# Row maxima that start with the first 512 keys, later zeros, and value products handed out one and a half batches per turn

## The chip, the core and the metric

The kernel runs on one core of a Trainium2 chip. The core has a matrix engine (PE; its weight loads are listed apart as PEld), a vector engine (DVE), a scalar engine (ACT), a general engine (POOL) and a queue engine (SP) that issues transfers. Transfers (DMA) can also be issued from ACT and POOL. The measure is the device time of one launch in microseconds (us); lower is better.

## The reference

For 2048 tokens `x` of width 448 the kernel computes a gated mix of an attention block and an MLP block:

```python
g = sigmoid((x * gate_w).sum(-1, keepdims=True))
q, k, v = split_heads(x @ wqkv)                 # 16 heads of 28
scores = einsum("bhqd,bhkd->bhqk", q, k) * 28 ** -0.5
a = merge_heads(softmax(scores) @ v) @ wo
y = layernorm(x)
b = gelu(y @ w1 + b1) @ w2 + b2                 # 448 -> 1792 -> 448
return g * a + (1 - g) * b
```

All data are float32. The softmax subtracts the maximum of each row of scores, so the maximum over all 2048 keys must be known before a row's exponentials are taken.

## The kernel before, in words

**Stages.** The program has three stretches. A short head loads the first inputs. The *strips* stretch computes the queries and keys (pieces `QK`), the values (`Val`) and the MLP (`Up`, then `Down`, for each of four chunks of 512 tokens). The *attention* stretch computes scores, exponentials and the products with the values, and ends with the output projection.

**Strips.** In the strips stretch PE is used as four strips of 32 rows. Four small products, one in each strip, run beside one another; a full product of 128 rows is cut into four pieces that visit the four strips. Class `Strips` is a planner that runs while the program is built: it keeps a modelled time for each strip (`t`), for DVE, ACT and POOL, and for the transfers (`get`: data at 230 GB/s, then 2.2 us), and writes the instructions in the order in which they come due. Everything that is to be done at a modelled time is put on a list with `at`. The engines then run this order at their own pace: each engine works its instructions strictly in order, and waits where an input is not there.

**Row maxima.** To have the maxima early, the scores are computed twice. The first time (`RowMax`) each of 1024 *searches* (`one`) multiplies 128 queries with 512 keys of one head in one strip (line L199), and a DVE reduction (L201) takes the maximum of each row. A search needs the keys of its head in `kd` and the queries in `qd`, both read back from DRAM, where the `QK` pieces wrote them (`qk<-qo`, issued by ACT). There are 16 rounds of 64 searches, one for each group of four heads and chunk of 512 queries. In the strips stretch searches go into strips wherever the planner finds one of the two score banks 6 and 7 free; what is left is done in the attention stretch. `hot[j]` is the modelled time from which strip j may search; `ready(j)` tells whether its keys are loaded.

Before the change, all four heads' whole keys (224 KB each) and queries (56 KB each) were loaded by POOL after the last key piece of all four chunks was done. For later groups the planner allowed the strip again 8.0 us after its last search with the old keys.

**Attention.** The 1024 units (128 keys by 512 queries of one head) are done in *turns* of 5 or 6 units. A turn writes, on PE: the scores of half a (three units, banks 0 to 2), those of half b (two or three units, banks 3 to 5), three products for each unit (L1121), with searches between them; then *batches* of value products (L1133), each of four units, into bank 7; then, late in the program, a piece of the output projection (L970 to L972, 12 products). ACT takes the exponentials of each half with one instruction (L1125) into a tile `p`; only then can the next turn's scores use the banks. A turn has 5 units with three searches while searches are owed, and 6 units with at most two after that: `turn_of` decides by what is left. Value batches are written as soon as the units of earlier turns make up four, so turns of six have one and two batches in turn.

**The end of the strips.** `early` prepares the attention while the last chunk of the MLP is still running: POOL zeroes `la`, fetches keys and queries and splits them into high and low parts.

## Time and profile before

| | us |
|---|---|
| median of 3 runs | 1094.24 (1091.7 to 1096.02) |
| the profiled execution, its own time | 1093.73 |
| its span | 1091.6 |
| first strip matmul / end of the strips / first exponential | 16.05 / 446.6 / 449.44 |
| searches before 449.44 us / after | 529 / 495 |

The span is what the trace covers. A *group* row gives the busy time and the mean duration of all instructions of one line; the *chain* is the path of work that ended last, followed back from the end; a row of *windows* gives, for a stretch of time, each engine's busy time and number of instructions; the *timeline* gives instructions in order of time, and in brackets the idle time ahead of one and what ended it. Several PE instructions in different strips or columns run beside one another, so PE is shown busy wherever at least one runs, and its share does not tell how many strips are filled. In the trace a float32 value product shows as two matmul instructions: a batch of four products is 8 of them.

### The profile page before, as it was taken

The page shows a single profiled execution, that of the slowest core. Times are in us where ns is not written, and L with a number is a line of the kernel's source. Part 1 is how long each engine was busy: PE and PEld are TensorE (multiplying, and loading weights), DVE is VectorE, ACT ScalarE, POOL GpSimd, SP SyncE. Part 2 cuts the span into 40 slices and gives each one's busy share as a digit, 9 for nine tenths or more (in the row PEclk, how much of TensorE's full clock was granted, in tenths as well). Part 3 has the DMA queues.
Part 4 walks back from the last instruction along what each step waited for, and adds up shares of the span by engine and source line. Part 5 has one row for each costly group of instructions (what it writes and reads, how often), then busy time and mean ns, then how long its engine had stood idle before and what let it go on. Part 6 is the DMA issues. An engine that isn't in the chain of part 4 may idle for free.

```text
span 1091.6 us, 30496 instructions
## 1 busy us (share of the span) xinstructions
PE 1074.6 (98%) x13170; PEld 724.8 (66%) x13170; DVE 739.2 (68%) x1186; ACT 634.8 (58%) x668; POOL 364.1 (33%) x372
## 2 busy tenths in 40 slices
PE   9999999999999999999999999999999999999998
PEld 7989999999999999644444444444444444354555
DVE  4289989998999998667666766566767666321102
ACT  5324472141151150588878878878878878858562
POOL 3546687345242057321100110310012215345441
PEclk9999999999999999999999999999999999999999
DMA  6795433104100105410000000400002101011111
GB/s 231 225 293 190 167 120 109 43 5 103 38 9 11 38 9 127 119 40 27 18 14 19 22 23 25 117 17 16 19 18 73 38 16 54 25 52 38 61 52 59
DMA packets 47462, 73.15 MB, mean 67 GB/s; under 512 B 13632, under 2 KB 28608, under 8 KB 46416
## 3 DMA queue, kind: packets, MB, share of 16 engines
q1 hardware_dynamic: 33888, 39.11, 12.4%
q0 software_dynamic: 4800, 16.89, 5.4%
q10 hardware_dynamic: 8640, 15.21, 3.9%
q8 instruction: 103, 1.69, 0.6%
q14 instruction: 31, 0.25, 0.1%
HBM read 51.75 MB, written 19.31 MB: 65 GB/s over the span
## 4 chain that ended last, share of the span: by engine, by line
PE 93%; ACT 2%; DVE 2%; issue 1%; DMA 1%; POOL 0%; DVEq 0%; ACTq 0%
PE bk L475 33%; PE bk L1133 22%; PE bk L1121 18%; PE bk L199 15%; ACT p L1125 2%; PE bk L970 1%; DVE mx L201 1%; PE bk L971 1%; PE bk L972 1%; PE bk L886 1%; DMA qk<-qo 1%; PE bk L871 0%; DVE ob L992 0%; POOL hl L350 0%; DVE acc L977 0%
## 5 line engine op out<-in xcount | busy, mean ns | idle before, releaser
L201 DVE TENSOR_REDUCE mx<-bk 128x1 f32<-128x512 f32 x1024 | 672.4, 689 | 202.8 <-PE bk L199 157.0
L1125 ACT ACTIVATE p<-bk 128x1536 f32<-128x1536 f32 (+1 forms) x395 | 482.1, 1276 | 142.2 <-PE bk L1121 142.2
L199 PE MATMUL bk<-kd,qd 28*128 28x512 f32 x1024 | 446.7, 437 | 3.7 <-issue 1.4
L199 PEld LDWEIGHTS bk<-kd,qd 28*128 28x128 f32 x1024 | 186.1, 182 | 196.9 <-DVE mx L201 131.8
L475 PE MATMUL bk<-yh,w1f 32*128 32x512 f32 x1568 | 183.0, 391 | 0.4 <-ACT gb L385 0.4
L475 PE MATMUL bk<-yl,w1f 32*128 32x512 f32 x784 | 161.0, 391 | 0.0
L475 PEld LDWEIGHTS bk<-yh,w1f 32*128 32x128 f32 x1568 | 151.8, 183 | 2.2 <-ACT gb L385 1.7
L475 PE MATMUL bk<-w2h,hh 32*128 32x448 f32 x896 | 133.2, 366 | 1.3 <-ACT hh L343 1.3
L475 PE MATMUL bk<-w2l,hh 32*128 32x448 f32 x896 | 132.5, 363 | 0.0
L1133 PE MATMUL bk<-p,va 128*32 128x512 f32 x1024 | 131.2, 602 | 0.0
L1133 PE MATMUL bk<-p,vb 128*32 128x512 f32 x1024 | 129.5, 601 | 0.0
L350 POOL TENSOR_TENSOR hl<-h,hh 128x512 fp32r<-128x512 f32 x56 | 73.7, 1325 | 132.2 <-ACT hh L343 71.2
L806 POOL CAST yh<-yl 128x512 fp32r<-128x512 f32 x16 | 9.8, 614 | 293.6 <-PE bk L1133 118.4
L1121 PE MATMUL bk<-yh,ka 29*128 29x512 f32 x512 | 107.0, 482 | 0.3 <-ACT h L385 0.3
L475 PEld LDWEIGHTS bk<-yl,w1f 32*128 32x128 f32 x784 | 103.6, 183 | 0.2
L1121 PE MATMUL bk<-yh,kb 29*128 29x512 f32 x512 | 98.1, 477 | 3.8 <-ACT p L1125 3.5
L475 PEld LDWEIGHTS bk<-w2h,hh 32*128 32x128 f32 x896 | 99.5, 183 | 1.9 <-ACT hh L343 1.7
L475 PEld LDWEIGHTS bk<-w2l,hh 32*128 32x128 f32 x896 | 100.4, 183 | 0.1
L1121 PE MATMUL bk<-yh,la 28*128 28x512 f32 x512 | 88.5, 393 | 0.0
L385 ACT ACTIVATE gb<-bk 128x448 f32<-128x448 f32 x14 | 7.6, 545 | 138.3 <-PE bk L475 133.3
L475 PE MATMUL bk<-w2h,hl 32*128 32x448 f32 x896 | 87.3, 362 | 0.0
L1121 PE MATMUL bk<-yl,ka 28*128 28x512 f32 x512 | 86.9, 410 | 0.0
(141 smaller groups left out, 1591.3 us busy)
## 6 DMA issues: line engine op xcount, KB each, us to landing
qk<-qo ACTq DMA_DIRECT2D x28, 256.0 KB
raw<-in_xt SPq DMA_DIRECT2D x17, 256.0 KB
vs<-vt ACTq DMA_DIRECT2D x16, 256.0 KB
rc<-rls SPq DMA_DIRECT2D x60, 64.0 KB
bxr<-in_xk POOLq DMA_DIRECT2D x8, 448.0 KB, 6.4
acc<-gbs SPq DMA_DIRECT2D x16, 224.0 KB
out_y<-acc SPq DMA_DIRECT2D x16, 224.0 KB
qd<-qk SPq DMA_DIRECT2D x60, 56.0 KB
```

Source lines behind the costliest of these rows:

```text
L199: nc.tensor.matmul(ps, self.qd[n % 2][r, i * P:(i + 1) * P], self.kd[r, k * 512:(k + 1) * 512], start=True, stop=True)
L201: nc.vector.reduce_max(self.mx[n % 2][:, j, i, k:k + 1], ps, axis=AX)
L350: nc.gpsimd.tensor_sub(hl[f], h, hh[f].bitcast(F32))
L475: mm = nc.tensor.matmul(bk[:, x.bank, :n], a, b, start=x.first, stop=(len(x.rem) == 1 and m == len(ops) - 1), skip_group_check=True)
L806: nc.gpsimd.tensor_copy(h, l.bitcast(F32))
L886: nc.tensor.matmul(bk[:, b], w, v, start=(i == 0), stop=(i == len(ops) - 1), skip_group_check=True)
L970: nc.tensor.matmul(po, h, woh[:, g], start=(g == 0), stop=False, skip_group_check=True)
L971: nc.tensor.matmul(po, h, wol[:, g], start=False, stop=False, skip_group_check=True)
L972: nc.tensor.matmul(po, l, woh[:, g], start=False, stop=(g == NG - 1), skip_group_check=True)
L1121: nc.tensor.matmul(bk[:, turn_bank(i)], w[r, ks], q[r], start=(p == 0), stop=(p == 2), skip_group_check=True)
L1125: nc.scalar.activation(t[:, :count], bk[:, b:b + count], AF.Exp, scale=SCALE)
L1133: nc.tensor.matmul(bk[32 * j:32 * j + 32, 7], vg[n // NC][:, k, 32 * j:32 * j + 32], prob.pop(4 * b + j), start=(k == 0), stop=(k == NT - ...
```

## The change

1. **Key blocks.** `load_block(c)` loads the 512 keys of chunk c for the four heads of the first group (four transfers of 28x512, 56 KB each) on POOL's queue. It is called 4.0 us (modelled) after the strips begin for chunk 0, together with the first queries, and for each later chunk 5.0 us after the two pieces that hold those keys. The first round goes through the keys outermost, so that it can begin with one block; `ready` lets it go as far as `blocks` says.
2. **Allowed from the modelled landing.** For later groups `hot[j]` is set when the keys' transfer is issued, to its modelled landing plus 1.0 us, and the transfer is entered in the planner's model of the transfers.
3. **Zeros later.** In `early`, the zeroing of `la` moves from 0.5 to 4.0 us after the last `Up` piece, the key fetches by 2.5 us and their splits by 1.5 us.
4. **Half batches.** In a turn of six, value work is limited to a quota of 3 halves (4 when more than two batches are behind). A batch may be cut into two halves of 256 columns, the second of which is written in the next turn.

```diff
         def ready(self, j):
-            n = self.cnt[j] // 16
+            n, x = divmod(self.cnt[j], 16)
+            if n == 0:
+                return x // 4 < self.blocks
...
-            i, k = divmod(x, 4)
+            i, k = divmod(x, 4) if n else divmod(x, 4)[::-1]
...
                 elif kind == "k":
-                    self.at(now + 1.5, lambda n=n, j=j: rowmax.load_k(n, j))
-                    self.hot[j] = now + 8.0
+                    def load(n=n, j=j):
+                        rowmax.load_k(n, j)
+                        self.hot[j] = self.get(self.clock + 0.6, 224) + 1.0
+
+                    self.at(now + 1.5, load)
+                    self.hot[j] = 1e9
...
+            if x.i in (3, 4) and all((x.c, m) in st.qks for m in (3, 4)):
+                keys(st, x.c, now + 5.0)
             if not st.keyed and all((c, m) in st.qks for c in range(NC) for m in (3, 4)):
                 st.keyed = True
-                def first(j):
-                    rowmax.load_k(0, j, nc.gpsimd)
-                    rowmax.load_q(0, j, nc.gpsimd)
...
+    def keys(st, c, when):
+
+        def load():
+            if c == 0:
+                for j in range(4):
+                    rowmax.load_q(0, j, nc.gpsimd)
+                    st.use("pool", st.clock, 0.55)
+                    st.get(st.pool, 56)
+            rowmax.load_block(c, nc.gpsimd)
+            st.use("pool", st.clock, 0.6)
+            st.at(st.get(st.pool, 230) + 1.0, landed)
+
+        def landed():
+            rowmax.add_block()
+            st.hot = [min(x, st.clock) for x in st.hot]
+
+        st.at(when, load)
...
+        keys(st, 0, 4.0)
...
-        st.at(now + 0.5, lambda: nc.gpsimd.memset(la.bitcast(F32), 0.0), pool=2.2)
+        st.at(now + 4.0, lambda: nc.gpsimd.memset(la.bitcast(F32), 0.0), pool=2.2)
...
-    def batch(b, turn):
+    def batch(b, turn, sl=slice(0, CH)):
...
-        before = u
+        before, quota = u, 99
         if u < UNITS:
             u += turn_of(u, turn)
+            if u - before == 6:
+                quota = 3 + (before // 4 - b > 2)
...
-        while 4 * b + 4 <= before:
-            b += 1
-            if batch(b - 1, turn):
+        while 4 * b + 4 <= before and quota:
+            if quota == 1 and not begun_half:
+                if b % NT:
+                    batch(b, turn, slice(0, CH // 2))
+                    begun_half = True
+                break
+            last = batch(b, turn, slice(CH // 2 if begun_half else 0, CH))
+            quota -= 1 if begun_half else 2
+            b, begun_half = b + 1, False
+            if last:
                 break
```

What this does to the order of the instructions is shown at three places. The first is POOL's queue early in the strips stretch: `first` and `raw` are landing buffers for inputs and weights, `bxr` those of the layer statistics, `wq` the split weights of the `QK` pieces. Before:

```order
L554 DMA first_136<-in_xt 128x512
L554 DMA first_137<-in_wqk 128x512
L554 DMA raw_130<-in_wqk 128x512
L96 TENSOR_TENSOR wq_526<-first_137,wq_526 128x384
L97 TENSOR_TENSOR wq_526<-first_137,wq_526 64x128
L96 TENSOR_TENSOR wq_549<-raw_130,wq_549 128x384
L97 TENSOR_TENSOR wq_549<-raw_130,wq_549 64x128
L554 DMA bxr_147<-in_xk 128x2x448
L554 DMA bxr_148<-in_xk 128x2x448
L554 DMA raw_131<-in_wqk 128x512
```

Now, from the same transfer on:

```order
L571 DMA first_136<-in_xt 128x512
L196 DMA qd_150<-qk 28x512 x4
L186 DMA kd<-qk 28x512 x4
L571 DMA first_137<-in_wqk 128x512
L571 DMA raw_130<-in_wqk 128x512
L96 TENSOR_TENSOR wq_536<-first_137,wq_536 128x384
L97 TENSOR_TENSOR wq_536<-first_137,wq_536 64x128
L96 TENSOR_TENSOR wq_561<-raw_130,wq_561 128x384
L97 TENSOR_TENSOR wq_561<-raw_130,wq_561 64x128
L186 DMA kd<-qk 28x512 x4
L571 DMA bxr_147<-in_xk 128x2x448
L571 DMA bxr_148<-in_xk 128x2x448
```

Twenty small loads now stand among the early transfers (a row with x4 is four of them): four of queries and four of the first key block ahead of the next weights, and a block of four ahead of the statistics' inputs, twice more further down. Before, eight loads (four of 28x2048 keys, four of 28x512 queries) stood together further down the queue, behind the loads of two later sets of `QK` weights.

The second place is PE in the attention stretch, where turns of six without searches stand. `yh`, `yl` are the split queries, `kb`, `lb` the split keys, `vb` the values, `p` the exponentials. Before, with the value batches of one turn (four products), the scores of the next, and its batches (eight products):

```order
L1133 MATMUL bk<-p_15797,vb 32x512
L1133 MATMUL bk<-p_15832,vb 32x512 x3
L1121 MATMUL bk<-yh,kb 128x512 x3
L1121 MATMUL bk<-yh,lb 128x512 x3
L1121 MATMUL bk<-yl,kb 128x512 x3
L1121 MATMUL bk<-yh,kb 128x512 x3
L1121 MATMUL bk<-yh,lb 128x512 x3
L1121 MATMUL bk<-yl,kb 128x512 x3
L1133 MATMUL bk<-p_15843,vb 32x512 x3
L1133 MATMUL bk<-p_15866,vb 32x512 x3
L1133 MATMUL bk<-p_15877,vb 32x512 x2
```

Now, from the second part of one turn's value work on (half a batch of 256 columns), the scores of the next turn, and its value work (half a batch and a whole one):

```order
L1164 MATMUL bk<-p_15987,vb 32x256
L1164 MATMUL bk<-p_15998,vb 32x256 x3
L1152 MATMUL bk<-yh,kb 128x512 x3
L1152 MATMUL bk<-yh,lb 128x512 x3
L1152 MATMUL bk<-yl,kb 128x512 x3
L1152 MATMUL bk<-yh,kb 128x512 x3
L1152 MATMUL bk<-yh,lb 128x512 x3
L1152 MATMUL bk<-yl,kb 128x512 x3
L1164 MATMUL bk<-p_15987,vb 32x256
L1164 MATMUL bk<-p_15998,vb 32x256 x3
L1164 MATMUL bk<-p_16024,vb 32x512 x3
L1164 MATMUL bk<-p_16035,vb 32x512
```

Most turns of six (49 of 57) now have one and a half batches behind their scores, where one and two took turns. Over the whole stretch the order has 161 turns of five and 36 of six before and a last one of three units, with 495 searches; now 136 of five, 57 of six and a last one of two, with 458 searches. 28 batches are cut in two. Of the 57, 28 hold two searches.

The third place is POOL at the end of the last `Up` pieces (`hl` is the low part of the MLP's hidden layer, needed by `Down`). Before:

```order
L350 TENSOR_TENSOR hl_2821<-h,hh_2807 128x512
L829 MEMSET la 128x2048
L350 TENSOR_TENSOR hl_2822<-h,hh_2808 128x512
L350 TENSOR_TENSOR hl_2823<-h,hh_2809 128x512
L350 TENSOR_TENSOR hl_2824<-h,hh_2810 128x512
L802 DMA yl<-qk 28x512
L785 DMA la<-qk 28x2048
```

Now:

```order
L363 TENSOR_TENSOR hl_2912<-h,hh_2898 128x512
L363 TENSOR_TENSOR hl_2911<-h,hh_2897 128x512
L363 TENSOR_TENSOR hl_2913<-h,hh_2899 128x512
L833 DMA yl<-qk 28x512
L860 MEMSET la 128x2048
L833 DMA yl<-qk 28x512
L816 DMA la<-qk 28x2048
```

The zeroing of `la` stood ahead of the last three low parts and now stands behind them, after the first query fetch.

More of the change, by code (lines that the diff above doesn't have):

```diff
@@ L169, in __init__ @@
             self.has = set()
+            self.blocks = 0
             self.qd = [mpool.tile([P, CH], F32R, name=f"qd{i}") for i in range(2)]
@@ L180, in load_k, with load_block, add_block @@
             self.has.add((g, j))
+        def load_block(self, c, queue):
+            cs = slice(c * CH, (c + 1) * CH)
+            for j in range(4):
+                queue.dma_start(self.kd[32 * j:32 * j + DH, cs].bitcast(F32), qk[D + j * DH:D + (j + 1) * DH, cs])
+        def add_block(self):
+            self.blocks += 1
+            if self.blocks == NC:
+                self.has.update((0, j) for j in range(4))
         def load_q(self, n, j, queue=nc.sync):
@@ L736, in done @@
                 early(st, now)
+    def keys(st, c, when):
+        def load():
+            if c == 0:
+                for j in range(4):
+                    rowmax.load_q(0, j, nc.gpsimd)
[8 more added lines that the diff above has]
+        st.at(when, load)
     def enter_mlp(st, now):
```

12 lines of the change are left out of this document (5 added, 7 removed).

## Prediction

> **What bounds the kernel.** I read the page first, then the groups, then windows and the chain for each stretch.
>
> ```profile
> span 1091.6 us, 30496 instructions
> PE 1074.6 (98%) x13170; PEld 724.8 (66%) x13170; DVE 739.2 (68%) x1186; ACT 634.8 (58%) x668; POOL 364.1 (33%) x372
> DVE  4289989998999998667666766566767666321102
> PE 93%; ACT 2%; DVE 2%; issue 1%; DMA 1%; POOL 0%; DVEq 0%; ACTq 0%
> ```
>
> PE is busy everywhere and carries 93% of the chain, at the full granted clock in the windows below. So time is gained only by PE's rows being fewer, being filled better in their four strips, or not standing still. DVE is nearly full from 57 us to the end of the strips (446 us), and has room before and behind. Where searches can be done is therefore a question of DVE's room in the strips.
>
> ```profile
> 20.00:57.00 37.00, 37.00 (x628) 36.87 (x625) 8.16 (x20) 10.23 (x19) 16.52 (x27) 1.00 0.64 195
> 57.00:446.00 389.00, 384.35 (x6623) 368.90 (x6617) 363.91 (x580) 125.68 (x223) 194.12 (x186) 1.00 0.29 89
> 449.44:920.57 471.13, 378.78 (x320) 1.00 0.13 37
> 920.57:1066.60 146.03, 99.06 (x73) 1.00 0.13 43
> 920.57:1066.60 146.03, 17.26 (x44) 8.24 (x44) 1.00 0.13 43
> ```
>
> The first two rows are windows of all engines (columns: width, then busy time and count of PE, PEld, DVE, ACT, POOL). From 20 to 57 us DVE works 8.16 of 37 us: this is the hole into which the change puts searches. The next two rows count the exponentials, two to a turn: 320 of them are 160 turns in 471.13 us, 2.945 us for a turn of five, chunk changes included. The last row counts line L970, four to a piece of the output projection: 11 pieces.
>
> **Fewer and other turns.** The order has 25 turns of five fewer (161 to 136) and 21 turns of six more (36 to 57). The fives go with 25 x 2.945 = 73.6 us; between chunk changes a turn is a little shorter, as four turns in the chain show, 638.36 - 626.68 = 11.68 or 2.92 each:
>
> ```profile
> 626.68 1.85 PE bk L1133 x16
> ...
> 638.36 1.90 PE bk L1133 x16
> ```
>
> I take 2.92: 73.0 us. What a turn of six costs depends on its value batches.
>
> ```profile
> 944.07 1.85 PE bk L1133 x16
> 945.92 0.92 PE bk L1121 x11
> ...
> 948.28 1.46 ACT p L1125
> 949.77 0.51 PE bk L1121 x3
> ...
> 950.75 1.85 PE bk L1133 x16
> ...
> 957.43 1.85 PE bk L1133 x16
> ```
>
> This is the chain through two pairs of turns of six. From one double batch (x16) to the next it is 6.68 us, and in each pair the chain leaves PE: the exponentials of half b end at 949.74, and only then PE writes the next scores of half b. The turn with one batch is too short for ACT, the turn with two leaves ACT idle. Where nothing waits, the parts are these:
>
> ```profile
> 990.32 1.85 PE bk L1133 x16
> 992.18 1.60 PE bk L1121 x16
> ...
> 1013.23 0.99 PE bk L1133 x8
> ...
> 932.50 0.42 PE bk L199
> ...
> 934.22 1.00 PE bk L1133 x8
> ```
>
> Scores of six units take 1.60 us, with two searches 934.22 - 932.50 = 1.72. One batch takes 0.99, a second behind it 0.86, so half a one 0.43. A turn with one and a half batches is then 1.60 + 0.99 + 0.43 = 3.02 us, or 3.14 with two searches. ACT needs less:
>
> ```profile
> 946.93 5.48 ACT L1125 ACTIVATE p<-bk 128x1536 f32<-128x1536 f32 x4 [1.20 <-PE bk L1121]
> ```
>
> Four exponentials back to back take 5.48, 2.74 for a turn; the 1.20 us of idleness ahead of them is what an even share takes away. The scores of that turn began at 945.92, so the exponentials start 1.01 after a turn's scores and both have ended 1.01 + 2.74 = 3.75 after them. Half b of the next turn is due 3.02 + 0.92 = 3.94 after them. The banks are free 0.2 us early: little, and the reason for the second rival.
>
> Now the sum for the sixes. The window of 146.03 us holds 35 of the 36 sixes, one five and 11 projection pieces. A piece is the gap between a batch and the next scores:
>
> ```profile
> 1014.22 0.40 PE bk L970
> ...
> 1016.85 1.59 PE bk L1121 x16
> ```
>
> 2.63 us. So a six costs (146.03 - 2.92 - 11 x 2.63) / 35 = 3.26 us on the mean, 36 of them 117.4. After it 28 with two searches make 87.9 and 29 others 87.6, together 175.5. The 28 cut batches issue twice as many products; between nothing (the second half starts behind other products) and 0.13 each (what a batch that comes first pays over one that follows) that is 0 to 3.6, and I take 1.0, since a half mostly follows a whole batch. In "TensorE: Matmul & The Clock Gate", section Back-to-back issue gap, the Trainium skill gives 518 cycles for 512 columns and 262 for 256, so that cutting would cost 6 cycles a product; by that this term would be about 0.1 and the time 0.9 lower. No run here shows a product of 256 columns. Attention: 175.5 + 1.0 - 117.4 - 73.0 = -13.9.
>
> **The searches that move.** 37 more searches stand in the strips.
>
> ```profile
> 30.00:40.00 10.00, 10.00 (x178) 10.00 (x174) 1.51 (x4) 2.68 (x5) 5.85 (x9) 1.00 0.74 224
> 57.54 2.58 DVE L201 TENSOR_REDUCE mx<-bk 128x1 f32<-128x512 f32 x4 [8.65 <-PE bk L475]
> ```
>
> With full strips 178 products start in 10 us, so one costs 0.056 us: +2.1. Their reductions, 2.58 / 4 = 0.65 each, 24 us, are covered by DVE's hole. If that cover is gone, they queue as searches do now, and PE stands.
>
> **Two places where PE stood still.**
>
> ```profile
> 262.00:266.00 4.00, 2.58 (x51) 2.21 (x46) 2.30 (x5) 0.00 (x0) 0.00 (x0) 1.00 0.98 201
> 264.64 0.47 PE L199 MATMUL bk<-kd,qd 28*128 28x512 f32 x1 [1.42 <-issue]
> 257.83 1.37 SPq L179 DMA_DIRECT2D kd<-qk  x1
> 407.00:411.00 4.00, 2.67 (x51) 2.26 (x51) 2.30 (x4) 2.61 (x4) 3.41 (x4) 1.00 0.03 8
> 405.23 1.50 POOL la L829
> 407.00 1.31 POOL hl L350
> 408.33 0.70 ACT h L342
> 427.87 1.29 POOL L791 TENSOR_TENSOR la<-la,ka 128x512 fp32r<-128x512 f32 x1
> ```
>
> At 263 us PE idles 1.42 us ahead of a search: its last key set was issued at 257.83, into transfers 0.98 busy, and the strip was allowed 8.0 us after its last search. The change waits for the modelled landing, and the second group's keys now come 50 searches earlier, away from those input loads: -1.4. At 408 us the chain runs through the zeroing of `la` (1.50), then a low part, then ACT, then PE, which idles 4.00 - 2.67 = 1.33. The zeros now stand behind the low parts; what they delay next, the key splits, end with the row of 427.87, 17 us before the strips do: -1.3. Next in line at both places are the low parts and DVE, which were not late. Bounds for the two: 0 to 2.7.
>
> **Transfers and POOL.** Twelve more issues of about 0.51 us are 6.2 us of POOL, ahead of weights that POOL splits.
>
> ```profile
> 30.59 1.01 POOL L96 TENSOR_TENSOR wq<-first,wq 128x384 fp32r<-128x384 f32 x1 [11.23 <-ACT wq L92]
> qd<-qk POOLq DMA_DIRECT2D x4, 56.0 KB, 6.3
> kd<-qk POOLq DMA_DIRECT2D x4, 224.0 KB, 6.3
> DMA to landing us min/median/max: 3.6/6.3/7.9
> ```
>
> POOL stands idle 11.23 us at that place, so the issues cost nothing there, and the other two blocks go into similar holes (16.52 of 37 us busy). What can cost is the landing. 56 KB and 224 KB took the same 6.3 us. The first search of a block holds up PE's queue, with all four strips behind it. Between the best and the worst landing of the keys lie 7.9 - 3.6 = 4.3 us; the first block is read into transfers that are quiet then, so I take 1.0 for all blocks, between 0 and 4 x 4.3 = 17.2. The Trainium skill speaks against small loads: "DMA: Bandwidth & Descriptors", section Bandwidth, says that transfers under 64 KB are dominated by descriptors, and gives 2.0 us fixed for each. If four of a block paid that one after another, a block would land 6 us later than a single load. The two rows above, equal for a fourth of the bytes, say that they overlap; no run here shows four of 56 KB alone.
>
> **Sum.** -13.9 + 2.1 - 1.4 - 1.3 + 1.0 = -13.5, from 1093.73 us, the profiled execution's own time (its span and 2.1 us around it, and 0.5 below the median): 1080.2.
>
> **Rivals.**
>
> *Late statistics hold the searches, and it gets slower.* Statistics loads and searches share DVE's queue:
>
> ```profile
> DVE stt L130 <- DMA bxr<-in_xk: 20.5, 4, 15.2
> ```
>
> Before, DVE waited 20.5 us for these inputs with no search behind it. Now most of the 64 searches of the first round stand between them, and the inputs are issued later, behind key blocks. With two banks, PE gets two searches further and then stands, all strips. If the whole 20.5 us falls on PE, the time is 1080.2 + 20.5 = 1100.7. It ends slower than before from 13.5 us on, and slower by over 0.5% from 19. Against it: 15.2 of the 20.5 lie ahead of the first input, where DVE now has searches to do.
>
> *The half batches don't bring the exponentials in time.* Half b is due only 0.2 us behind its banks. If sixes stay at 3.26, attention gives 57 x 3.26 = 185.8 instead of 175.5, and the time is 1090.5. Against it: turns that wait for nothing, as at 992 us, exist.
>
> *The strips eat part of it.* Forward searches meet DVE's work at other places, where the first round's searches share it with the inputs' low parts and the statistics. Three to five standstills like the two above, of 1.4 us each, give 4.2 to 7.0 us, 1084 to 1087. For it speaks that DVE has no other free stretch ahead of 446 us; against it that the hole, 28.8 us, holds the 24 us.
>
> **Chances.** Forecast 0.62 (by itself 1075 to 1084), strips eat part 0.18, no gain from halves 0.12, late statistics 0.08. A difference under 0.5% (5.5 us) can't be told from none. Faster by more: 0.62 + 0.18 = 0.80 and 0.01 of the case without gain from halves, 0.81; within it 0.11; slower by more 0.08. The range takes in that case with 2.5 us of landing behind it, and below it the lower bounds: halves and landings at nothing (-2.0), moved searches that find unfilled strips and cost nothing (-2.1), fives at 2.945 (-0.6). That is 1075 to 1093.
>
> **What the next profile shows if this is right.** 387 exponentials; sixes at 3.0 to 3.15 without the leaps of the chain to L1125; DVE's slices 2 and 3 fuller; no idleness of PE ahead of the first search with new keys and none behind the zeros; the first exponential within 2 us of 449.4. Wrong would be: PE waits on a first search between 27 and 60 us, DVE waits on `bxr` with searches behind, turns of six over 3.25, or a first exponential later than 452.

## The result, and the profile after

The changed kernel takes 1094.01 us (median of 22 runs, 1089.26 to 1096.66), the kernel before 1094.37 beside it. The ratio is 0.9994, with an interval from 0.9984 to 1.0004: no difference that can be measured. The forecast was 1080.2 us, and the time lies outside its range of 1075 to 1093. The profiled execution took 1093.69 us, its span is 1091.9.

The page of the changed kernel, in the lines that answer to those shown of the kernel before:

```profile
span 1091.9 us, 30966 instructions
PE 1074.4 (98%) x13394; PEld 728.4 (67%) x13394; DVE 740.4 (68%) x1186; ACT 634.0 (58%) x660; POOL 368.7 (34%) x384
DVE  4899898898999999866776665667676544311102
PE 95%; ACT 1%; DMA 1%; DVE 1%; issue 1%; SPq 0%; DVEq 0%; ACTq 0%
```

DVE's second slice, 27 to 55 us, has filled from 2 to 8 tenths, as it should. The page alone gives little hint of what went wrong: SPq is new in the chain, and in its list of the chain by line the writes `vs<-vt` and `gbs<-gb` stand with 1% each, where neither stood before. The windows say more (all engines; width, then busy time and count of PE, PEld, DVE, ACT, POOL, then the granted clock, the share and the rate of the transfers):

```profile
20.00:57.00 37.00, 37.00 (x616) 36.06 (x613) 28.76 (x51) 10.71 (x19) 23.62 (x41) 1.00 0.59 189
57.00:456.88 399.88, 393.25 (x6703) 374.85 (x6696) 370.10 (x590) 126.96 (x227) 192.36 (x185) 0.99 0.28 87
456.88:855.25 398.37, 319.58 (x270) 1.00 0.13 37
```

In the hole from 20 to 57 us DVE now works 28.76 us in place of 8.16, and PE never stops there. But the first exponential comes at 456.88 us, 7.44 later than before, and the granted clock in the strips is 0.99 where it was 1.00. The last row counts the exponentials of the turns of five: 270 of them, 135 turns, 2.951 us for a turn. From the first exponential to the end it is 635.03 us, 7.18 less than before (642.21). So what attention gained, the strips lost.

**What the strips lost.** PE's waits in the strips, by who ended them (total, times, longest):

```profile
PE bk L488 <- ACT gb L398: 2.5, 2, 1.4
PE bk L488 <- SPq L529: 2.2, 1, 2.2
PE bk L488 <- ACT zall L325: 1.9, 1, 1.9
```

None of these three stood among the long ones before. The waits at the keys (263 us) and behind the zeros (408 us) are gone, as forecast. In place of them PE stands still at 107, 189, 296 and 379 us. From here on a standstill is counted from the start of the last product ahead of it to the start of the next one; where nothing waits that is 0.06 us. (The idle time of the rows above begins at the modelled end of the last product and is about 0.36 us shorter.) The chain through the first (start, length, what):

```profile
101.26 0.06 PE bk L488
...
101.41 7.29 DMA vs<-vt
...
108.77 0.07 ACT vt L324
...
109.22 0.17 ACT zall L325
...
109.43 0.47 PE bk L488
```

ACT brings each value group into one of three buffers `vt` and writes it to DRAM. The write issued at 101.41 landed 7.29 us later, in the middle of the five loads that POOL issued from 99.48 to 101.82 us (transfers 0.98 busy from 104 to 108). ACT waited for it:

```profile
108.77 0.54 ACT L324 ACTIVATE vt<-bk 128x448 f32<-128x448 f32 x1 [6.83 <-DMA vs<-vt]
```

One of the three buffers was free by then: its write, issued at 98.40, had landed at 100.59, by the trace's record of its semaphore. But the buffer goes by the group's number (`vt[self.i % 3]`), the planner closes group 6 ahead of group 5, and the buffer of group 6 is the one whose write for group 3 went out at 101.41. So its bank stayed full, and PE stood for 2.26 us. At 189 us the chain leaves by another way. This is SP's queue there:

```profile
184.56 0.34 SPq L196 DMA_DIRECT2D qd<-qk  x1
187.96 2.58 SPq L569 DMA_DIRECT2D raw<-in_xt  x4
190.65 0.98 SPq L196 DMA_DIRECT2D qd<-qk  x1
```

L529 is no transfer: when a piece passes from one strip to the next, SP raises a semaphore for which the next strip's product waits. SP works in order. Ahead of the hand-off stand four loads of inputs, 2.58 us to issue, and one of queries, 0.98 us where the same issue took 0.34 at 184.56. No product starts on PE from 189.16 to 191.74, 2.58 us. At 296 and 379 us ACT waits for a `gbs` write of 2.83 and 3.89 us, with two buffers `gb` for it.

**What a standstill costs behind itself.** PE alone, around the first two standstills (width, busy time, count, granted clock, transfers):

```profile
107.00:109.50 2.50, 0.60 (x15) 1.00 0.71 273
109.50:113.50 4.00, 4.00 (x48) 0.57 0.40 150
113.50:117.50 4.00, 4.00 (x74) 1.00 0.35 133
...
189.00:192.00 3.00, 0.78 (x13) 0.95 0.79 206
192.00:195.00 3.00, 3.00 (x34) 0.50 0.89 287
```

Behind each of the two, the granted clock is 0.50 for 3.4 us in all, and as many products take twice the time: 1.71 us lost each time, 3.42 together, as the sum of windows of 1 us gives it. Before the change the clock stands at 1.00 throughout, though PE stood for 1.77 us at 263 us. The first wait of 2.26 us thus cost 4.0, the second of 2.58 cost 4.3.

From the first strip product (started at 15.98 us before, 16.68 now) to the first exponential it was 433.46 us before and is 440.20 now, 6.74 more (the other 0.70 lies in the head, which varies by as much between runs). 37 searches at 0.058 us (87.00 us for 1500 products, from 20 to 107 us) make 2.1; the standstills over 0.45 us add up to 8.32 where they were 6.77 (the two priced ones and four of 0.7 to 1.2 us, which went too), 1.6 more; the clock makes 3.4. That is 7.1 for the 6.74 measured.

**What attention gained.** The 57 turns of six, with 12 projection pieces among them, take 213.3 us (36 took 148.6, with as many pieces); the 136 fives 402.3 (161 took 474.1). So sixes cost 64.7 more, where 59.1 was forecast, and the fives give 71.8, where 73.0 was. The chain through plain turns, and through the place where a new chunk of queries begins:

```profile
1033.09 1.80 PE bk L1152 x12
1034.90 1.43 PE bk L1164 x16
1036.32 1.60 PE bk L1152 x14
1037.93 1.43 PE bk L1164 x16
1039.35 1.81 PE bk L1152 x18
```

```profile
873.89 1.08 PE bk L1152 x13
...
875.20 0.61 PE bk L1164 x8
...
875.82 1.45 ACT p L1156
...
877.32 0.50 PE bk L1152 x3
```

One and a half batches take 1.43 us, 0.99 and 0.43 as worked out: the cut itself costs nothing. The term of 1.0 for it was not needed, and the estimate from the Trainium skill's page ("TensorE: Matmul & The Clock Gate", Back-to-back issue gap, 262 cycles for 256 columns beside 518) agrees with these rows. But every second score stretch takes 1.80 and not 1.60: PE waits 0.2 us inside it, for the banks that the 0.2 of margin in the prediction was to keep free. The exponentials still set the pace there, though the chain does not show waits this short: those of the turn begun at 1033.02 end at 1036.90, and the first product into the banks of half b starts at 1036.96; those of the turn begun at 1036.25 end at 1040.13, and it starts at 1040.18. Two such turns take 6.26 us, 3.13 each. And where one batch and then two still come in turn, at the chunks' borders, the chain goes through the exponential as before. PE also waits for DVE twice, for a search behind a projection piece:

```profile
PE bk L212 <- DVE acc L1008: 1.7, 2, 0.8
```

Mean without the pieces' 2.63 us each: (213.3 - 12 x 2.63) / 57 = 3.19 us for a six, forecast 3.10 with the cuts.

### The profile page after: what moved, and what is told of

Its sections match the earlier page's. It is cut to its first block, busy times and chain, and to the rows that moved or that the text cites. A ratio compares the mean times of both kernels' runs of the same rounds, so it can differ in the third digit from the quotient of the medians.

```text
span 1091.9 us, 30966 instructions
## 1 busy us (share of the span) xinstructions
PE 1074.4 (98%) x13394; PEld 728.4 (67%) x13394; DVE 740.4 (68%) x1186; ACT 634.0 (58%) x660; POOL 368.7 (34%) x384
## 4 chain that ended last, share of the span: by engine, by line
PE 95%; ACT 1%; DMA 1%; DVE 1%; issue 1%; SPq 0%; DVEq 0%; ACTq 0%
PE bk L488 34%; PE bk L1164 22%; PE bk L1152 19%; PE bk L212 15%; PE bk L1001 1%; PE bk L1002 1%; PE bk L1003 1%; ACT p L1156 1%; PE bk L917 1%; DMA vs<-vt 1%; DMA gbs<-gb 1%; PE bk L902 0%; DVE ob L1023 0%; PE bk L945 0%; DVE acc L1008 0%
## 5 line engine op out<-in xcount | busy, mean ns | idle before, releaser
L488 PE MATMUL bk<-yh,w1f 32*128 32x512 f32 x1568 | 188.6, 393 | 2.5 <-ACT gb L398 2.5
L488 PE MATMUL bk<-yl,w1f 32*128 32x512 f32 x784 | 164.2, 393 | 0.0
L488 PE MATMUL bk<-w2h,hh 32*128 32x448 f32 x896 | 140.6, 368 | 2.2 <-SPq L529 2.2
L488 PE MATMUL bk<-w2l,hh 32*128 32x448 f32 x896 | 140.0, 366 | 0.0
L1164 PE MATMUL bk<-p,va 128*32 128x512 f32 (+1 forms) x1080 | 130.6, 579 | 0.0
L1164 PE MATMUL bk<-p,vb 128*32 128x512 f32 (+1 forms) x1192 | 129.4, 540 | 0.0
L1152 PE MATMUL bk<-yh,ka 29*128 29x512 f32 x512 | 104.3, 481 | 0.6 <-ACT p L1156 0.6
L488 PEld LDWEIGHTS bk<-w2h,hh 32*128 32x128 f32 x896 | 102.2, 185 | 3.3 <-SPq L529 2.6
L1152 PE MATMUL bk<-yh,la 28*128 28x512 f32 x512 | 86.3, 392 | 0.0
```

The costliest lines, as they stand in the source:

```text
L488: mm = nc.tensor.matmul(bk[:, x.bank, :n], a, b, start=x.first, stop=(len(x.rem) == 1 and m == len(ops) - 1), skip_group_check=True)
L1152: nc.tensor.matmul(bk[:, turn_bank(i)], w[r, ks], q[r], start=(p == 0), stop=(p == 2), skip_group_check=True)
L1164: nc.tensor.matmul(bk[32 * j:32 * j + 32, 7, sl], vg[n // NC][:, k, 32 * j:32 * j + 32], prob[4 * b + j][:, sl], start=(k == 0), stop=(k = ...
```

## The experiments

All were timed beside the kernel before, whose median was between 1093.6 and 1094.5 in these groups. What each left in its profiled execution stands in one table: searches ahead of the first exponential, the sum of PE's standstills over 0.45 us there (what lies above the usual 0.06), the time that the half clock cost there, the length of the strips (first strip product to first exponential) and of attention.

| kernel | searches | standstills | half clock | strips | attention |
|---|---|---|---|---|---|
| before | 529 | 6.8 | 0 | 433.5 | 642.2 |
| changed | 566 | 8.3 | 3.4 | 440.2 | 635.0 |
| halves alone | 529 | 6.5 | 1.7 | 434.9 | 640.2 |
| blocks alone | 572 | 10.3 | 5.1 | 443.4 | 637.6 |
| zeros alone | 531 | 4.8 | 0 | 431.8 | 642.2 |
| landing rule alone | 537 | 4.9 | 0 | 433.6 | 642.9 |
| halves and zeros | 531 | 3.6 | 0 | 429.8 | 640.5 |
| changed, first round held | 536 | 4.5 | 1.7 | 434.6 | 637.9 |
| changed, late loads on POOL | 566 | 9.1 | 1.7 | 439.6 | 634.3 |
| changed, four buffers `vt` | 566 | 6.9 | 0 | 435.7 | 633.7 |
| changed, four buffers, POOL | 566 | 7.0 | 0 | 436.2 | 633.2 |
| changed without landing rule | 572 | 10.4 | 5.1 | 443.6 | 631.7 |
| the same, four buffers `vt` | 572 | 7.0 | 1.7 | 438.0 | 630.4 |
| before, four buffers `vt` | 529 | 5.2 | 0 | 432.7 | 643.8 |

The first three columns of numbers explain the fourth: 433.5 plus 0.058 for each search more, plus the standstills' and the clock's difference, gives every strip length within 1.6 us, nine of the thirteen within 0.8.

### The four parts, each by itself

Half batches in the kernel before, nothing else (the new `batch` and its loop):

```diff
+            if u - before == 6:
+                quota = 3 + (before // 4 - b > 2)
...
+                    batch(b, turn, slice(0, CH // 2))
+                    begun_half = True
```

> The kernel before with part 4 alone (half batches in turns of six). The strips stretch has the same order as before, so the first exponential should stand within 0.7 us of 449.4. Theory A (what the changed kernel's profile suggests: half batches cost nothing and take away most waits of PE for the exponentials): the 36 turns of six held 11 long score stretches (2.1 to 2.25 us instead of 1.60 to 1.72), 6.2 us of waiting; about half of that goes, 1091 us. Rival (half batches only move the wait): within 1 us of before.

Measured: 1091.87 us, ratio 0.9988 [0.9974, 1.0001], alone not clear of noise. Attention is 2.0 us shorter; 36 sixes at 3.10 in place of 3.26 would be 5.8. The sixes take 142.8 us in place of 148.6, but with one projection piece of 2.63 fewer, so 3.2 less; from the first score of the last turn to PE's last product it is 18.94 us in place of 15.39, that piece included, so 0.9 more. In this execution the old standstill on the keys (2.39 us) drew the half clock behind it:

```profile
262.00:266.00 4.00, 1.97 (x41) 1.00 0.98 192
266.00:270.00 4.00, 4.00 (x48) 0.58 0.57 164
```

Key blocks alone:

```diff
             if x.i in (3, 4) and all((x.c, m) in st.qks for m in (3, 4)):
                 keys(st, x.c, now + 5.0)
-                    self.hot[j] = self.get(self.clock + 0.6, 224) + 1.0
+                    self.hot[j] = now + 8.0
...
(halves and zeros as before)
```

> The kernel before with part 1 alone (row maxima by key blocks). Theory A (the searches done early save turns of five, and the strips stretch gives all of it back, since every transfer after the blocks stands at another place): 387 exponentials or about so, first exponential 5 to 9 us later than 449.4, attention 4 to 8 us shorter, total 1092 to 1097. Rival B (the blocks cost the strips only the 2.1 us of the searches, and the loss comes from the landing rule or the zeros): first exponential 2 to 3 us later, total about 1088.

Measured: 1097.44 us, ratio 1.0028 [1.0014, 1.0042], slower. 43 searches more stand ahead of the first exponential, and attention is 4.6 us shorter: 66 sixes take 249.2 us (36 took 148.6) and 125 fives 368.9 (161 took 474.1). The strips are 10.0 us longer. The standstill at the value rows is 4.45 us here, and the clock falls for two stretches of 3.4 us behind it. The blocks are the part that brings the loss.

Zeros later, alone:

```diff
-        st.at(now + 0.5, lambda: nc.gpsimd.memset(la.bitcast(F32), 0.0), pool=2.2)
+        st.at(now + 4.0, lambda: nc.gpsimd.memset(la.bitcast(F32), 0.0), pool=2.2)
```

> The kernel before with part 3 alone (zeros of la behind the last low parts). The chain showed PE idle for 1.33 us behind the zeros. If nothing else waits there: first exponential 1.3 us earlier, total 1092.9. Rival (the last hidden tiles are late for another reason, or the order behind it shifts): within 0.5 us of before.

Measured: 1092.34 us, ratio 0.9987 [0.9977, 0.9998], 1.3 us, as priced. The standstill of 1.68 us at 408 us is gone, and nothing took its place.

The landing rule alone:

```diff
-                    self.hot[j] = now + 8.0
+                        self.hot[j] = self.get(self.clock + 0.6, 224) + 1.0
```

> The kernel before with part 2 alone (keys of later groups used from the modelled landing). PE stood 1.42 us ahead of a search with new keys at 263 us. Theory A: this wait goes, total 1092 to 1093, if the order behind it doesn't meet other transfers. Rival B (this rule causes the strips' loss of the changed kernel): first exponential 3 us or more later than 449.4.

Measured: 1096.27 us, ratio 1.0030 [1.0017, 1.0043], slower. The wait that it was to remove stays: 1.71 us at 260.5 us and 0.67 at 264, still at searches with new keys. In the order before, the keys of that place are loaded into transfers that are 0.98 busy (258 to 262 us); that the planner's modelled landing comes too early there is read from this and wasn't tried apart. The profiled execution is longer by 0.2 us in the strips and 0.7 in attention only, and its time of 1095.09 is one of the shorter of its runs; what the rest of the 3 us is, this run does not tell.

### Are the searches or the transfers to blame?

Late loads on POOL's queue in place of SP's, in the changed kernel:

```diff
                 if st.late:
-                    nc.sync.dma_start(t, src)
+                    nc.gpsimd.dma_start(t, src)
```

> The changed kernel, with the feeder's late loads issued by POOL in place of SP, in the same order. Theory A (the strips lose their time to transfers that are issued or signalled late): the standstill of PE at 189 us, 2.58 us with a second of 0.53 behind it, is there because the hand-off signal of the second split stands on SP's queue behind four late loads, each of which took 0.34 to 0.92 us to issue. With the loads on POOL it goes: 2.5 to 3 us less, about 1091.2 us, the first exponential at about 454. Theory B (the 37 searches more that stand ahead of the first exponential cost more than their own 0.058 us each, wherever the transfers lie): the standstill only moves, and the time stays at 1094.

Measured: 1092.72 us, ratio 0.9987 [0.9975, 0.9999]. The standstill at 189 us is gone, so it was the hand-off in SP's queue. But the time falls by half of what was expected, since three others came at 148, 166 and 178 us (2.24, 0.87 and 0.81). At 148 us PE waits for a maximum from DVE. DVE and POOL there:

```profile
144.84 1.38 DVE L214 TENSOR_REDUCE mx<-bk 128x1 f32<-128x512 f32 x2
146.13 3.56 DVE L153 TENSOR_TENSOR w2l<-raw,w2h 128x448 fp32r<-128x448 f32 x1
```

```profile
145.00 0.55 POOL L569 DMA_DIRECT2D raw<-in_w  x1
145.57 2.55 POOL L363 TENSOR_TENSOR hl<-h,hh 128x512 fp32r<-128x512 f32 x2
148.07 1.13 POOL L153 TENSOR_TENSOR w2l<-raw,w2h 128x448 fp32r<-128x448 f32 x1
```

The low part of a weight block takes DVE 0.61 us where nothing disturbs it. Here it takes 3.56, from 146.13 to 149.69, and ends 0.49 us behind the last of POOL's three instructions in a row (148.07 + 1.13), which like it read two inputs. That POOL held it is read from these rows and wasn't tried apart. The searches' maxima queue behind it, and with both score banks full PE stops. (That these are waits for queries, as the expectation of the last run of this part has it, was misread: PE waits for the maxima.)

Four value-row buffers in place of three, in the changed kernel:

```diff
-    vt = [px.tile([P, H, 32], F32, name=f"vt{i}") for i in range(3)]
+    vt = [px.tile([P, H, 32], F32, name=f"vt{i}") for i in range(4)]
...
-            v, ps, tt = vt[self.i % 3], bk[:, self.bank], self.i
+            v, ps, tt = vt[self.i % 4], bk[:, self.bank], self.i
```

> The changed kernel with four value-row buffers in place of three, so that ACT waits for the write of four groups earlier. Theory A: the standstill of 2.26 us at 107 us, where ACT's eviction waited for a value-row write and PE for the bank, shrinks to under 0.6 us: 1.7 to 2.2 us less, about 1092. Theory B: PE stands still elsewhere instead, and the time stays at 1094.

Measured: 1089.74 us, ratio 0.9959 [0.9945, 0.9973], 4.3 us less than the changed kernel, twice what was expected. The standstill shrinks from 2.26 to 0.98 us, and the clock does not fall:

```profile
110.73 0.33 PE bk L488 x5
111.06 0.63 issue
111.69 1.29 PE bk L488 x18
```

The standstill at the hand-off is still there, 2.26 us at 188 us, and in this execution the clock stays at 1.00 behind it too. The strips are 2.25 us longer than before: the 37 searches make 2.1 of it, and the standstills add up to what they were (6.9 and 6.8).

The same four buffers in the kernel before, as a control:

```diff
-    vt = [px.tile([P, H, 32], F32, name=f"vt{i}") for i in range(3)]
+    vt = [px.tile([P, H, 32], F32, name=f"vt{i}") for i in range(4)]
```

> The kernel before with four value-row buffers in place of three, nothing else: the control for the fourth buffer. Theory A (the wait for the value-row writes is made by the searches that now stand among the early strips): the kernel before has no standstill at its value rows, so the fourth buffer changes nothing: 1094, within 1 us. Theory B (the fourth buffer helps whatever the searches do, and the changed kernel's gain with it is the buffer's own): 2 to 4 us less, 1090 to 1092.

Measured: 1095.1 us, ratio 1.0014 [1.0005, 1.0022]: no gain, rather 1 us more. The fourth buffer is worth something only where the moved searches stand.

The first round's searches held back until all four blocks are there; the loads stay where the change put them:

```diff
         def landed():
             rowmax.add_block()
-            st.hot = [min(x, st.clock) for x in st.hot]
+            if rowmax.blocks == NC:
+                st.hot = [min(x, st.clock) for x in st.hot]
```

> The changed kernel, in which no search of the first round begins until all four key blocks have landed; the blocks are loaded as early as in the changed kernel. Theory A (what costs the strips is where the transfers now lie, the block loads among them): the standstills at 107 and 189 us stay, 1.5 us or more each, and the first exponential comes at 455 to 457. Theory B (the searches among the early strips push the rest): the searches ahead of the first exponential fall back towards 529, the first exponential comes at 450 to 452, and the turns after it lose what they had gained: 1094 again, by a later first search and fewer turns of six saved.

Measured: 1092.52 us, ratio 0.9986 [0.9973, 0.9999]. The second theory holds for the strips (not for the time, which it put at 1094: attention keeps 4.3 us of its gain): 536 searches, the first exponential at 451.94 us, DVE's hole empty again, and no standstill of PE at 107 or 189 us, though the blocks are loaded as early as in the changed kernel:

```profile
20.00:57.00 37.00, 37.00 (x621) 36.73 (x624) 7.86 (x18) 11.31 (x21) 23.89 (x41) 1.00 0.68 211
...
107.00:109.50 2.50, 2.50 (x52) 1.00 1.03 397
109.50:113.50 4.00, 4.00 (x78) 1.00 0.52 194
187.00:192.00 5.00, 5.00 (x102) 1.00 0.11 33
```

The transfers around 107 us are as busy (1.03), but PE's work there is not the same. So the loads of the blocks bring neither of these standstills; with the searches put ahead the planner's pieces fall elsewhere, and value groups and hand-offs meet the full queues. Why just these pieces fall there, the runs don't tell: the planner decides that by its modelled times. Nor do they tell what 1.3 us of the strips here are, the part that the table's sum leaves over. The old wait on the keys is back (2.99 us at 261 us, the half clock behind it).

Both aids, POOL and the fourth buffer, in the changed kernel:

```diff
-                    nc.sync.dma_start(t, src)
+                    nc.gpsimd.dma_start(t, src)
...
-            v, ps, tt = vt[self.i % 3], bk[:, self.bank], self.i
+            v, ps, tt = vt[self.i % 4], bk[:, self.bank], self.i
```

> The changed kernel with four value-row buffers and the late loads issued by POOL: of the five standstills in its strips the one at 107 us should shrink to under 1 us, as with the four buffers alone, and the one at 189 us go, as with POOL alone. If POOL's queue then holds the query loads again (three standstills of 2.24, 0.87 and 0.81 us on the searches' queries at 148 to 178 us, as with POOL alone), it gives 1089.5 to 1091, no better than the four buffers alone (1089.74); else about 1087.

Measured: 1089.76 us, ratio 0.9966 [0.9954, 0.9977], no better than the fourth buffer alone. The waits at 107 and 189 us are gone, those for DVE's maxima (2.25, 0.86, 0.81) stand again.

### What a standstill costs

In the kernel before, DVE copies the value tile of the next batch onto itself four times ahead of turn 60; the output does not change:

```diff
+        if turn == 60:
+            v = vg[b // NT // NC]
+            for _ in range(4):
+                nc.vector.tensor_copy(v, v)
```

> The kernel before with one standstill put in on purpose: ahead of turn 60 of attention, DVE copies the value tile that the next batch reads onto itself four times, so that the batch, and PE behind it, waits. How long S the standstill is, the trace shows; by DVE's rows it should lie between 2.5 and 7 us. Theory H (a standstill of over about 2.3 us also costs the clock: in the changed kernel the granted clock was 0.50 for 3.4 us behind the standstills at 107 and 189 us): the clock is 0.50 for 3.4 us or more behind it, and the time is S + 1.7 longer than before. Theory N (a standstill costs itself): the clock stays at 1.00 and the time is S longer.

Measured: 1100.52 us, ratio 1.0060 [1.0039, 1.0082], 6.6 us more; attention 6.34 us longer.

```profile
626.00:631.00 5.00, 0.72 (x8) 0.72 0.00 0
631.00:635.00 4.00, 4.00 (x19) 0.50 0.01 2
635.00:639.00 4.00, 4.00 (x45) 1.00 0.00 0
```

DVE copies from 625.11 to 630.12 us, a search's maximum queues behind the copies, and PE waits for it: no product starts from 626.10 to 630.77 us, and PE idles 4.28 us of that. The clock falls inside the standstill, about 2 us after its beginning, and comes back at 635.0, two times 3.4 us later. PE runs 4.3 us of that at half speed and loses 2.1: 4.3 + 2.1 = 6.4, where attention is 6.34 longer. The clock's part is shown, and the standstill alone would have cost 4.3.

Over all profiled executions the clock fell behind every one of seven standstills of 2.53 us or more and behind none that was shorter than 1.9. Of those between, it fell behind 2.26, 2.39 and 2.42 us, and behind 1.91 with 0.47 right after it; it did not behind 2.49, 2.26, 2.25, 2.24 and 2.11, nor behind four of 1.91 to 1.96.

What tells them apart is in the traces. In each run all changes of the clock lie whole multiples of 3.413 us apart (in the changed kernel 102.4, 3.41, 78.5 and 3.41 us, from 7.39 us on: 30, 1, 23 and 1 times). Cut every run, from 20 to 1075 us, into such steps. In twelve steps PE idled 1.89 us or more, and each time the clock was 0.50 in the next step; behind steps with 1.42 us or less it never was; of the five between, with 1.53 to 1.70, two drew the fall. The standstill of 2.49 us lay across the border of two steps, with 1.33 us of idleness in the fuller one; the one of 2.26 us at 107 us lay in one step, with 1.90. So the same wait draws the fall or not by where it lies on this grid.

The Trainium skill, in "TensorE: Matmul & The Clock Gate", Part 1 on the clock gate, says that the clock is halved after an idle window of about 3.4 us and that the window runs freely. The length of the fall, 3.4 us or twice that, and the fixed steps agree; that the whole window must be idle does not: here 1.89 us in one was enough. The changed kernel's spread goes with this: its shortest run, 1089.26 us, is the only one of the 22 with a mean granted clock of 1.000, and the eleven longest, from 1094.32 up, all lie at 0.997 or under.

### Versions that keep a gain

Half batches and later zeros in the kernel before, no blocks and no landing rule:

```diff
-        st.at(now + 0.5, lambda: nc.gpsimd.memset(la.bitcast(F32), 0.0), pool=2.2)
+        st.at(now + 4.0, lambda: nc.gpsimd.memset(la.bitcast(F32), 0.0), pool=2.2)
...
+                quota = 3 + (before // 4 - b > 2)
```

> The kernel before with the half batches and the later zeros alone; the key blocks and the landing rule stay as they were. Alone the one gave 0.9988 and the other 0.9987 of the time before. If what they save lies in different places (the zeros at 408 us, the halves behind the first exponential), they add: 0.9975, about 1091.2 against 1094. If the earlier first exponential takes searches from ahead of it and gives them back in turns of six, they don't: 0.999.

Measured: 1088.94 us, ratio 0.9951 [0.9934, 0.9968]. They add, and a bit more than add: the wait on the keys was only 1.30 us in this execution, and the clock stayed up.

The changed kernel with the landing rule undone:

```diff
-                        self.hot[j] = self.get(self.clock + 0.6, 224) + 1.0
+                    self.hot[j] = now + 8.0
```

> The changed kernel with the landing rule undone (a key set is used 8 us after its load again); blocks, zeros and halves stay. Alone the rule gave 1.0030 of the time before. Theory A (the rule only holds searches back, which then come in attention): 2 to 3 us less than the changed kernel, about 1091.5, with more searches ahead of the first exponential than 566. Theory B (in the changed kernel the rule is what keeps PE from the wait at 263 us, which is gone there): a standstill of 1.3 to 2.5 us on the keys comes back at 260 to 265 us, with 1.7 more if the clock falls behind it, and the time is 1094 to 1097.

Measured: 1090.10 us, ratio 0.9969 [0.9953, 0.9985], 3.9 us less than the changed kernel. The wait at 263 us does not come back: what removed it in the changed kernel was the place of the second group's keys, not the rule. Six searches more stand ahead of the first exponential, and attention is 3.3 us shorter (631.7): the rule held searches back into attention. The strips are the worst of all in this execution, 443.6 us with 5.1 of it by the half clock, and its time, 1093.09, is 3 us over the median of its runs.

The same with four value-row buffers:

```diff
-                        self.hot[j] = self.get(self.clock + 0.6, 224) + 1.0
+                    self.hot[j] = now + 8.0
...
-            v, ps, tt = vt[self.i % 3], bk[:, self.bank], self.i
+            v, ps, tt = vt[self.i % 4], bk[:, self.bank], self.i
```

> The changed kernel with the landing rule undone and four value-row buffers in place of three. If both act as by theory A, the fourth buffer takes 4.3 us off what the landing rule undone gives: about 1087. If the two interfere (another order of the transfers), it stays at 1089 to 1094.

Measured: 1086.34 us, ratio 0.9926 [0.9912, 0.9940], the lowest time of these versions, 7.6 us less than the kernel before. Against halves and zeros alone (0.9951) that is a little less, but the two intervals overlap, so what the blocks and the fourth buffer add is not settled. PE alone, at the place of the value rows and at the hand-off:

```profile
104.00:108.00 4.00, 4.00 (x79) 1.00 0.98 347
108.00:112.00 4.00, 3.01 (x54) 1.00 0.52 199
184.00:188.00 4.00, 2.62 (x48) 1.00 0.43 112
188.00:192.00 4.00, 3.31 (x34) 0.57 0.90 271
```

The first standstill is 1.34 us and draws nothing behind it; the one at the hand-off is 2.42 us, and the clock still falls behind it.

## Why the prediction was wrong, point by point

**The step "the searches that move" and the sum of the strips: wrong.** The prediction added +2.1 for the products, -1.4 and -1.3 for the two old waits and +1.0 for landings, +0.4 in all; measured were +6.74 in the strips and +7.44 at the first exponential. The searches' own price held (0.058 a search), and DVE's hole did hold them: PE never stops between 20 and 57 us. Both old waits went. What failed is "next in line are the low parts and DVE, which were not late". Next in line were a value-row write of 7.29 us, two `gbs` writes and a hand-off in SP's queue, none of which the prediction looked at. The moved searches change where every later piece of the planner falls, and these fell onto busy transfers and queues. 6.8 us of standstills became 8.3.

**A standstill was priced at its own length: wrong.** Two of the new ones halved the clock for 3.4 us each, 3.4 us of loss in the profiled execution, the largest term of all in the strips and one that the prediction didn't have. The rival "the strips eat part of it" named the mechanism, three to five standstills of 1.4 us (4.2 to 7.0 us), at 0.18. It had the number of them about right (four) and their net cost too small, as it took no price behind them.

**The landings: the term was not needed.** No standstill lies at a block's first search, and with the first round held the same loads left PE running. The 16 block loads of the changed kernel landed sooner than the prediction's 6.3 us:

```profile
DMA to landing us min/median/max: 2.0/2.7/4.1
```

The four of the first block, issued from 22.14 us on, had all landed at 25.7. The Trainium skill's 2.0 us fixed for a load ("DMA: Bandwidth & Descriptors", Anatomy of one DMA) agrees with the shortest; that four would pay it one after another, which the prediction weighed, is not what happened.

**The fives: right.** 161 became 136; they gave 71.8 us where 73.0 was forecast.

**The sixes: mechanism right, size off.** The turns were even, the chain no longer leaves PE for the exponential but at the chunks' borders, and a half batch costs half. But a six takes 3.19 us and not 3.10. The margin of 0.2 was misread: a turn's exponentials end 3.87 us after its first score and not 3.75, and the score stretch grows as soon as half b starts more than 0.70 us behind half a, not 0.92 (1.60 us with 0.70, 1.80 with 0.90). By 3.02 + 0.70 the banks were due 0.15 us before they came free. So every second plain turn waits 0.2 us for them, one-and-two pairs are left at the borders, and twice a search waits 0.8 us for DVE behind a projection piece. On 57 turns that is 5.6 us. What the halves are worth shows best between the blocks alone and the changed kernel without the landing rule, which differ in halves and zeros only: attention 637.6 and 631.7, 5.9 us on 66 sixes. The rival "the half batches don't bring the exponentials in time" was half right: of the 0.16 us that a six was to save, 0.07 came. Attention gave -7.2, forecast -13.9: 5.6 from the sixes, 1.2 from the fives.

**The landing rule: wrong.** It was credited with the wait at 263 us (-1.4). Undone, the wait stays away and attention gains 3.3 us; alone it makes the kernel slower. It held searches back (six more stand in the strips without it), which the prediction did not price.

**The zeros: right**, 1.3 us priced and 1.3 measured alone.

**Late statistics** did not happen: no wait of DVE for them with searches behind was seen, and PE did not stop there. Of the signs named for a wrong forecast, the one that came is the first exponential later than 452 us.

The total, in the prediction's own terms: -13.9 became -7.2, +0.4 became +7.4. They cancel, by chance, to within 0.3 us.

## What to carry to other kernels

Where a planner places work by modelled times, a part that moves work early moves everything behind it; price not only the moved instructions but the buffers and queues that later pieces share (here three write buffers and an in-order queue that carries both transfers and hand-offs), by asking which of them has a wait that is only just hidden. Price a standstill of PE of about 2 us or more at its length and, by where it falls, 1.7 us on top; here that was worth a buffer. A buffer that goes by an item's number and not by the order of use can be waited for while another is free. Try the parts of a change apart: here the zeros were a gain and the halves with them, the landing rule was a loss, and the blocks, a loss alone, stood in the fastest version with a buffer more.

## What the runs showed of the hardware that was not expected

The granted clock fell to 0.50 behind standstills of PE, for 3.4 us or twice that, in fixed steps of 3.413 us: always behind a step in which PE idled 1.89 us or more, never behind one with 1.42 or less. A transfer's issue on SP took 0.34 us at 184.56 us and up to 0.98 between 187.96 and 191.63, where five in a row stood ahead of a hand-off for 3.7 us. That busy transfers make it longer is not shown: a load into `raw` at 151.69 took 0.94 us where they were 0.21 busy (150.69 to 152.69). And a DVE instruction with two inputs took 3.56 us in place of 0.61 while POOL ran three such instructions in a row; both kernels with the late loads on POOL show it, with the same 3.56.
